# Fewer, wider filler products in the opening, and a new order of stores, loads and conversions in block 1

## The chip, the cores and the metric

The kernel runs on one core of a Trainium2 chip. A core has five engines that run at the same time: PE (TensorE, matrix products; its weight loads are listed as PEld), DVE (VectorE), ACT (ScalarE), POOL (GpSimd) and SP (SyncE, which here only issues DMAs). Each has its own instruction stream, in order, and they wait for one another by semaphores. Data comes from HBM by DMA. PE works from SBUF and writes to PSUM, which has few banks.

The metric is the device time of one execution in microseconds (us).

## The reference

Two layers, one after the other. The first is a retention recurrence over 4 batches, 8 heads, 768 steps and a head size of 64:

```python
for t in range(S):
    state = gamma * state + einsum('bhd,bhe->bhde', k[:, :, t], v[:, :, t])
    y[:, :, t] = scale * einsum('bhd,bhde->bhe', q[:, :, t], state)
```

Its output, seen as x with 3072 rows (tokens) and 512 columns, goes through a dense layer of width 2048 with the Mish activation and back to 512:

```python
h = x @ w_in
g = h * tanh(softplus(h))
out = g @ w_out
```

q, k, v, both weights and the output are 32-bit floats; the kernel computes in 16 bits with 32-bit sums.

## The kernel before

The 3072 rows are cut into 24 chunks of 128 steps. Block 0 has four chunks, each of the ten later blocks two (`BLOCKS`, `first`): block 1 has chunks 4 and 5, block 2 has 6 and 7, block 3 has 8 and 9, block 4 has 10 and 11. For a block, PE computes the products of the recurrence (scores L431 and outer products L438, later L519), then the first dense layer (`g1`, L608, eight steps u = 0 to 7 for a block of two), then the second (`seven`, L811: seven products of half matrices in place of eight, from sums of the operands that DVE makes in `sums_a`, `sums_b` and `sums_c`). The recurrence of the next blocks is woven in between: `get_ready(blk + 1)` is called behind step u = 5 of `g1` in blocks 1 to 3 and gives PE the outer products and scores of the next block (for chunks 8 and 9 that is in block 2).

What a chunk needs before PE can take it:

- `load`: three DMAs of 256 KB on SP's queue (q, k, v, L143). `load_to(g)` loads all chunks below g that are not yet loaded.
- `casts_qk` and `casts_v`: three scaled conversions to 16 bits on POOL (L376, L379, L384). `cast_to(g)` does them for all chunks below g not yet converted; `ncast` counts.
- `turn_by_dma`: a transposing DMA of the converted q and k (L389), issued by SP, which waits for POOL. It writes `qkt`, which scores read. `turn_next(g)` is `cast_to(g + 1)` and then `turn_by_dma(g)`; `turn_load(g)` is `turn_next(g)`, `turn_next(g + 1)` and `load_to(g + 4)`; `turn_both(g)` does both chunks of a block and ends with `load_to`.

The order is written by hand. Every engine gets its instructions in the order in which the program calls them, and SP is a single queue: what stands behind a DMA that waits, waits too. Outputs are collected in `stores` with a due step, and `store_due(u)` at the head of step u issues those that are due (L198). Output tiles `osb` have five buffers; block 0 makes four (`g2_out`), each later block two (`seven`), and a buffer is free again when its store has landed.

In block 1, `plan_of(1)` hangs `turn_next(8)` behind step u = 0 and `load_to(11)` behind u = 1. In `seven`, `cast_behind(1, 2)` follows `sums_b`: POOL first copies one element of the third sum (`summed`, L1119), so that it waits for DVE, and then converts chunks. Hooks in `seven` then issue the transposes.

The opening (`first_block`) starts with DMAs for the first q, k and v. Until those land and are converted PE has nothing of its own, and `spin(n, per)` gives it products of an identity matrix with itself (L402) into a PSUM tile that is overwritten later: n times 128 columns, `per` times 128 columns in one product, and `per` is 4 if it isn't given. The opening's own work is: turns by PE (`turn_first_q`, `turn_pair`, L219) which DVE or ACT copy to SBUF (L223, L225), scores (L294) that DVE masks (L299), outer products (L312), and the sums of both (L339, L348).

Of the kernel before, what the change touches and what calls it, by code (L numbers as in the profile page):

```python
# [16 lines left out]
def kernel(  # L17
# [20 lines left out]
    first = [sum(BLOCKS[:i]) for i in range(len(BLOCKS))]  # L38
# [82 lines left out]
    ONE, MIX = 3, 6  # L121
    nload, ncast = [0], [0]
# [22 lines left out]
    def load(g):  # L145
        room(g)
        for n in range(3):
            load_one(g, n, nc.sync)

    def load_to(g):  # L150
        while nload[0] < min(g, NCK):
            load(nload[0])
            nload[0] += 1
# [73 lines left out]
    def turn_first_q(qf, a, on_act):  # L227
        n = H // 2
        q16 = castp.tile([P, CPB, n, D], FP16, name="qk16", bufs=4)
        nc.vector.tensor_tensor(  # L230
            q16.rearrange("p r h d -> p h r d"), qf[:, a * n:(a + 1) * n],
            qs_four[:, a * n:(a + 1) * n].unsqueeze(3).broadcast_to((P, n, CPB, D)),
            op=ALU.mult)
        qt = qktp.tile([P, HP // 2, CPB, P], FP16, name="qkt", bufs=6)
        turn_parts(lambda i, r: q16[:, r, 2 * i:2 * i + 2], qt, on_act)
        first_q.append(qt)
# [29 lines left out]
    def turn_pair(n, nm, a, on_act):  # L266
        if a == 0:
            pairs[n, nm + "t"] = qktp.tile([P, HP, 2, C], FP16, name="qkt", bufs=6)
        t = pairs[n, nm, a]
        turn_parts(lambda i, r: t[:, r, 2 * i:2 * i + 2],  # L270
                   pairs[n, nm + "t"][:, a * (HP // 2):(a + 1) * (HP // 2)], on_act)
# [98 lines left out]
    def casts_qk(g):  # L370
        qf, kf, _ = loaded[g]
        qk16 = castp.tile([P, 2, H, D], FP16, name="qk16", bufs=4)
        q16, k16 = qk16[:, 0], qk16[:, 1]
        v16 = castp.tile([P, H, D], FP16, name="v16", bufs=7)
        heads = slice(g % 2 * (H // 2), (g % 2 + 1) * (H // 2))
        nc.gpsimd.tensor_tensor(  # L376
            q16.rearrange("p (r h) d -> p h r d", r=2), qf,
            qs_two[:, heads].unsqueeze(3).broadcast_to((P, H // 2, 2, D)), op=ALU.mult)
        nc.gpsimd.tensor_tensor(  # L379
            k16, kf, boosts.unsqueeze(2).broadcast_to((P, H, D)), op=ALU.mult)  # L380
        cast[g] = (q16, k16, v16, qk16)

    def casts_v(g):
        nc.gpsimd.tensor_tensor(  # L384
            cast[g][2], loaded.pop(g)[2], vs[g % 2].unsqueeze(2).broadcast_to((P, H, D)), op=ALU.mult)
# [11 lines left out]
    def spin(n, per=HP):  # L397
        at = pairs[min(x for x in pairs if type(x) is tuple and x[1] == "at")]
        to = at.rearrange("p h i r c -> p h (i r) c")
        for i in range(0, n, per):  # L400
            m = min(per, n - i)
            nc.tensor.matmul(  # L402
                to[:, 0, :m], ident, ident.unsqueeze(1).broadcast_to((P, m, P)),
                start=True, stop=True)
# [215 lines left out]
    def g2_mm(o_ps, blk, t, fb, cols=slice(None)):  # L620
        s, f = divmod(fb, FPS)
        nc.tensor.matmul(  # L622
            o_ps, gts[blk, fb][:, t * P:(t + 1) * P], wouts[s][:, f, cols],
            start=(fb == 0), stop=(fb == NFB - 1))

    def out_rows(blk, t):
        if blk == 0:
            return out[:TB].rearrange("(p r) c -> r p c", r=CPB)[t]
        row0 = (first[blk] + t) * P
        return out[row0:row0 + P]  # L630

    def g2_out(o_ps, t, due):
        osb = op.tile(list(o_ps.shape), FP32, name="osb", tag="osb")
        if t == 0:
            nc.scalar.copy(osb, o_ps)
        else:
            nc.vector.tensor_copy(osb, o_ps)
        stores.append((due, out_rows(0, t), osb))
# [265 lines left out]
    def first_block():  # L904
# [9 lines left out]
        pair_at(0, 0)  # L914
        spin(46, 1)
        turn_first_q(qf, 0, True)
        spin(14, 1)
        turn_first_q(qf, 1, False)
        for n in range(2):
            for a in range(2):  # L920
# [5 lines left out]
                base=0, pattern=[[-1, 2], [-2, D // 2]], channel_multiplier=1)  # L926
        keep_from(keep_two, 2, [[1, 2], [-1, 2], [-2, D]])
        turn_pair(0, "k", 0, True)
        spin(8, 1)
        pair_scores(0, 0)  # L930
        pair_at(0, 1)
        turn_pair(0, "k", 1, True)
        spin(8, 1)
        pair_scores(0, 1)
        turn_pair(1, "k", 0, True)
        cast_pair(0, "v", 0)
# [60 lines left out]
        def sum_weights(half, n):  # L997
# [5 lines left out]
        plan = {  # L1003
            9: [(cast_wout, 0)],
            12: [(cast_wout, 1)],
            16: [(cast_wout, 2), (load_more,), (cast_qk,)],
            17: [(sum_weights, 0, 3)],
            23: [(cast_wout, 3, True)],
            25: [(turn_two,)],
            26: [(pair_scores, 2, 0)],  # L1010
            27: [(pair_scores, 2, 1)],
# [5 lines left out]
        o_tiles = [None] * CPB  # L1017
        for u in range(2 * NFB):
            if u < 2:
                if u == 0:  # L1020
                    open_in(2)
            elif u < NFB:
                g1(0, u)
            elif u < 2 * NFB - 2:
                w = u - NFB
                if w == 0:
                    for t in range(CPB):
                        pool, tag = (pxps, "px") if t == 0 else (mmps, "mm")
                        o_tiles[t] = pool.tile([P, d_model], FP32, name="o_ps", tag=tag)
                for t in range(CPB):  # L1030
                    if t == CPB - 1 and w == 1:
                        g2_mm(o_tiles[t], 0, t, 0)
                    if t < CPB - 1 or w > 0:
                        g2_mm(o_tiles[t], 0, t, w)
            else:
                for t in range(CPB // 2) if u % 2 == 0 else range(CPB // 2, CPB):
                    for w in range(NFB - 2, NFB):
                        g2_mm(o_tiles[t], 0, t, w)
                    g2_out(o_tiles[t], t, 1)
            for fn, *args in plan.get(u + 1, ()):  # L1040
                fn(*args)

# [30 lines left out]
    def turn_both(g):  # L1073
        for n in range(2):
            casts_qk(g + n)
            turn_by_dma(g + n)
        for n in range(2):
            casts_v(g + n)
        ncast[0] = g + 2
        load_to(g + 4)  # L1080

    def next_chunk(g):
        turn_next(g)
# [32 lines left out]
    def cast_behind(blk, i):  # L1116
        g = first[blk] + (6 if blk == 1 else 8)
        if ncast[0] < min(g, NCK):
            nc.gpsimd.tensor_copy(summed, gsums[blk % 2][:, i, NFB // 2 - 1, P - 1:])  # L1119
            if blk + 1 >= MIX:  # L1120
                cast_to(g - 2)
                casts_qk(g - 2)
                ncast[0] = g
            else:
                cast_to(g)
# [5 lines left out]
    def plan_of(blk):  # L1131
        a = first[blk] + 4
        plan = {u: [] for u in (0, 1, 4, 5, 7)}
        if tight(blk):
            plan[5] = [(get_ready, blk + 1)]
        elif blk < MIX:
            plan[0] = [(settle, blk + 1), (mask_two, blk + 1), (leave, blk + 1)]
        if blk == 1:
            plan[0] += [(turn_next, a)]
            plan[1] += [(load_to, a + 3)]  # L1140
        elif blk < ONE:
            plan[1] += [(next_chunk, a)]
            plan[4] += [(load_to, a + 4)]
        return plan

    first_block()
    for blk in range(1, len(BLOCKS)):
        last = blk + 1 == len(BLOCKS)
        plan = plan_of(blk)
        if blk >= MIX:  # L1150
            second_of(blk - 1)
            mixed_in(blk, last)
        elif blk > ONE:
            weight_left.extend(in_sums(blk - ONE - 1))
        for u in range(NFB // 2 if blk < MIX else 0):
            store_due(u)
            g1(blk, u)
            if u in ((6, 7) if tight(blk) else (5, 7)):
                sums_a(blk, u // 7)
            for fn, *args in plan.get(u, ()):  # L1160
                fn(*args)
            if weight_left:
                weight_left.pop(0)()
        hooks = [[], [], []]
        if not last:
            later = blk + 2 if ONE <= blk < len(BLOCKS) - 2 else None
            hooks = [[(retain, blk + 1, later, True)],
                     [(next_one, first[blk] + 6)] if blk + 1 >= MIX else
                     [(next_two, first[blk] + 6, tight(blk))] if blk >= ONE else
                     [(turn_next, first[blk] + 5), (load_to, first[blk] + 8)] if blk == 1 else  # L1170
                     [(next_chunk, first[blk] + 5), (turn_load, first[blk] + 6)],
                     [(finish, blk + 1)] if later is None else []]
        if tight(blk):
            hooks[2].append((leave, blk + 1))
        seven(blk, [(mask_two, blk + 1)] if tight(blk) else [], hooks, last)
# [31 lines left out]
```

## Time and profile before

| what | us |
|---|---|
| median of 3 runs | 199.38 |
| all three | 199.31, 199.38, 200.82 |
| the profiled execution's own time | 200.37 |
| its span, first to last instruction | 198.6 |

| engine | busy us | share of the span | instructions |
|---|---|---|---|
| PE | 190.2 | 96% | 2999 |
| PEld | 154.8 | 78% | 2999 |
| DVE | 129.8 | 65% | 246 |
| ACT | 99.1 | 50% | 182 |
| POOL | 73.7 | 37% | 97 |

The profile is of one execution. Times in it count from the span's start. A row of a timeline gives start, length, engine, line and operation, output and inputs, shape and the number of merged instructions; in brackets stands how long the engine was idle before it, and what released it. "issue" there means that the engine waited for nothing that the profile shows. In the chain of waits each row is a start, a length and what the time went to. PE's products are pipelined and their ends are modelled, so distances from start to start are the surer measure.

The DMA engines are busy for 90% or more of nearly all slices up to 145 us.

### The profile page before, as it was taken

Reading aid. Unit: us, or ns where it says so; the run is one execution under the profiler, and the core shown is the slowest. Engines: PE = TensorE matmul, PEld = TensorE weight load, DVE = VectorE, ACT = ScalarE, POOL = GpSimd, SP = SyncE. Lnnn points to the kernel's source line nnn. Section 1 sums busy time; section 2 is a strip of 40 time slices with the busy share of each in tenths; the row PEclk is TensorE's granted clock in tenths of the full one; section 3 lists DMA queues with packets and bytes.
Section 4 is the critical chain, followed back from the end, with each engine's and each line's share of the span. In section 5 each row is a group of like instructions: output and inputs, shape, how many; then the busy total and the mean of one; then the engine's idle time right before and its main releaser. Section 6 shows DMA issues by size and latency. Waiting matters only on the chain.

```text
span 198.6 us, 6893 instructions
## 1 busy us (share of the span) xinstructions
PE 190.2 (96%) x2999; PEld 154.8 (78%) x2999; DVE 129.8 (65%) x246; ACT 99.1 (50%) x182; POOL 73.7 (37%) x97
## 2 busy tenths in 40 slices
PE   7799999999999999999799999999999999999993
PEld 7566444545887888888688888998998998988982
DVE  0688433988597269266946766866885884867462
ACT  2377673243642542554364464484484664763750
POOL 6562000659267603953905704434525710000000
PEclk9999999999999999999999999999999999999999
DMA  6999999999799999999999999879994250300202
GB/s 179 302 315 349 371 384 353 312 293 176 171 229 290 240 223 274 140 117 256 275 160 299 169 178 270 80 187 254 95 236 89 54 156 5 109 3 3 106 26 79
DMA packets 84141, 38.75 MB, mean 195 GB/s; under 512 B 57744, under 2 KB 78736, under 8 KB 84112
## 3 DMA queue, kind: packets, MB, share of 16 engines
q1 hardware_dynamic: 83968, 38.28, 82.2%
q8 instruction: 23, 0.38, 0.9%
q10 hardware_dynamic: 144, 0.05, 0.2%
q14 instruction: 6, 0.05, 0.1%
HBM read 27.31 MB, written 6.29 MB: 169 GB/s over the span
## 4 chain that ended last, share of the span: by engine, by line
PE 87%; DMA 5%; POOL 2%; DVE 2%; issue 2%; SPq 1%; ACT 1%; DVEq 0%; POOLq 0%
PE o_ps L811 29%; PE h_ps L608 23%; PE h_ps L738 9%; PE h_ps L718 8%; PE o_ps L622 7%; PE y_ps L519 3%; DMA kf<-in_k_dram 3%; DMA out_dram<-osb 2%; PE u_ps L438 1%; PE at L431 1%; PE t_ps L219 1%; PE at L294 1%; PE h_ps L593 1%; DVE am L299 1%; POOL v L384 1%
## 5 line engine op out<-in xcount | busy, mean ns | idle before, releaser
L608 PE MATMUL h_ps<-xt,win 128*128 128x256 f16 (+1 forms) x376 | 48.9, 289 | 1.3 <-issue 1.3
L616 ACT ACTIVATE g<-h_ps 128x512 f16<-128x512 f32 x54 | 32.3, 597 | 27.4 <-PE h_ps L608 27.4
L608 PEld LDWEIGHTS <-win 128*128 128x128 f16 x376 | 36.4, 98 | 12.1 <-issue 1.7
L811 PEld LDWEIGHTS <-gsum 128*128 128x128 f16 x320 | 30.1, 98 | 4.5 <-DVE gsum L681 0.7
L811 PE MATMUL o_ps<-tmat,gsum 128*128 128x256 f16 x240 | 29.4, 273 | 0.0
L811 PEld LDWEIGHTS <-g 128*128 128x128 f16 x240 | 23.2, 98 | 3.0 <-issue 0.4
L376 POOL TENSOR_TENSOR qk<-qf,qvs 128x512 f16<-128x512 f32 x18 | 19.5, 1083 | 8.7 <-DMA qf<-in_q_dram 4.7
L817 ACT COPY snap<-o_ps 128x256 f32<-128x256 f32 x30 | 11.2, 372 | 20.1 <-PE o_ps L811 20.1
L738 PE MATMUL h_ps<-xt,win 128*128 128x256 f16 x160 | 20.7, 273 | 0.0
L379 POOL TENSOR_TENSOR qk<-kf,qvs 128x512 f16<-128x512 f32 x18 | 19.7, 1093 | 0.0
L384 POOL TENSOR_TENSOR v<-vf,qvs 128x512 f16<-128x512 f32 x18 | 19.4, 1088 | 0.0
L811 PE MATMUL o_ps<-wout,g 128*128 128x256 f16 x160 | 19.1, 273 | 0.0
L825 DVE TENSOR_TENSOR osb<-o_ps,snap 128x256 f32<-128x256 f32 x30 | 12.7, 423 | 9.7 <-ACT xt L573 3.3
L1119 POOL COPY summed<-gsum 128x1 f16<-128x1 f16 x7 | 1.7, 245 | 40.6 <-DVE gsum L677 26.5
L738 PEld LDWEIGHTS <-win 128*128 128x128 f16 x160 | 14.8, 98 | 1.4
L573 ACT CAST xt<-y_ps 128x512 f16<-128x512 f32 x15 | 10.1, 731 | 10.9 <-PE y_ps L519 10.9
L729 ACT ACTIVATE g<-h_ps 128x512 f16<-128x512 f32 x25 | 14.2, 588 | 2.4 <-PE h_ps L738 2.4
L622 PE MATMUL o_ps<-wout,g 128*128 128x512 f16 x64 | 15.0, 380 | 0.0
L753 DVE TENSOR_TENSOR hsum<-h_ps,hsum 128x512 f32<-128x512 f32 x15 | 10.4, 692 | 6.1 <-PE h_ps L718 4.4
L748 ACT COPY hsum<-h_ps 128x512 f32<-128x512 f32 x15 | 8.8, 586 | 10.8 <-PE h_ps L718 10.8
L672 DVE TENSOR_TENSOR gsum<-g 128x512 f16<-128x512 f16 x20 | 9.1, 457 | 7.4 <-ACT g L616 5.3
L475 DVE TENSOR_TENSOR mid<-u_ps,sth 128x256 f16<-128x256 f32 x15 | 6.3, 422 | 9.8 <-PE u_ps L438 9.5
(97 smaller groups left out, 290.0 us busy)
## 6 DMA issues: line engine op xcount, KB each, us to landing
kf<-in_k_dram SPq DMA_DIRECT2D x24, 256.0 KB, 5.3
vf<-in_v_dram SPq DMA_DIRECT2D x24, 256.0 KB, 5.5
out_dram<-osb SPq DMA_DIRECT2D x22, 256.0 KB, 3.7
qf<-in_q_dram SPq DMA_DIRECT2D x20, 256.0 KB, 5.0
wi<-in_moe_w_in_dram SPq DMA_DIRECT2D x6, 512.0 KB, 8.5
wt<-in_moe_w_out_dram SPq DMA_DIRECT2D x3, 1024.0 KB, 10.4
qfirst<-in_q_dram SPq DMA_DIRECT2D x2, 512.0 KB, 4.5
wi<-in_moe_w_in_dram SPq DMA_DIRECT2D x1, 1024.0 KB, 10.0
```

The lines of the kernel that those rows point to most:

```text
L376: nc.gpsimd.tensor_tensor(q16.rearrange("p (r h) d -> p h r d", r=2), qf, qs_two[:, heads].unsqueeze(3).broadcast_to((P, H // 2, 2, D)), o ...
L379: nc.gpsimd.tensor_tensor(k16, kf, boosts.unsqueeze(2).broadcast_to((P, H, D)), op=ALU.mult)
L384: nc.gpsimd.tensor_tensor(cast[g][2], loaded.pop(g)[2], vs[g % 2].unsqueeze(2).broadcast_to((P, H, D)), op=ALU.mult)
L608: nc.tensor.matmul(h_ps[:, j], wins[s][f // 2][:, bp, f % 2 * P:(f % 2 + 1) * P], xts[blk][:, bp, :nt], start=(bp == 0), stop=(bp == NBP - 1))
L616: nc.scalar.activation(gt, h_ps, AF.Mish, scale=inv_boost3)
L622: nc.tensor.matmul(o_ps, gts[blk, fb][:, t * P:(t + 1) * P], wouts[s][:, f, cols], start=(fb == 0), stop=(fb == NFB - 1))
L718: nc.tensor.matmul(o_ps[:, f], w(f // 2, k)[:, f % 2 * P:(f % 2 + 1) * P], x[:, k], start=begin and f == 0 and k == 0, stop=k == 1, skip_g ...
L729: nc.scalar.activation(to, src, AF.Mish, scale=inv_boost3)
L738: nc.tensor.matmul(h_ps[:, f], wins[w][h // 2][:, k, h % 2 * P:(h % 2 + 1) * P], xts[blk][:, k, :2 * C], start=k == 0, stop=k == NBP - 1)
L811: nc.tensor.matmul(o_ps, x(f), w(f), start=first and z == 0, stop=z == n - 1, skip_group_check=True)
L817: nc.scalar.copy(x, o_ps)
L825: nc.vector.tensor_tensor(dst, o_ps, plus, op=ALU.add)
```

## The change

In the opening, three calls of `spin` take wider products: 14 products of 128 columns become 7 of 256, and twice 8 products of 128 become 2 of 512. The columns are the same, and there are 19 products, each with its weight load, fewer.

In block 1: block 0's four stores are due at step 0, not 1. `turn_both(6)` loads up to chunk 8 and not up to 9, and chunk 9 is loaded behind the stores, at step 0, in place of `turn_next(8)`. So chunk 8 is neither converted nor transposed there. `cast_behind(1, 2)` converts q and k of chunks 8 and 9 and then v of both, all behind the third sum; before, it converted chunk 9 alone. The hook that transposed chunk 9 now transposes 8 and 9. Nothing that is computed changes.

```diff
         turn_first_q(qf, 0, True)
-        spin(14, 1)
+        spin(14, 2)
         turn_first_q(qf, 1, False)
...
         turn_pair(0, "k", 0, True)
-        spin(8, 1)
+        spin(8)
         pair_scores(0, 0)
         pair_at(0, 1)
         turn_pair(0, "k", 1, True)
-        spin(8, 1)
+        spin(8)
         pair_scores(0, 1)
...
-                    g2_out(o_tiles[t], t, 1)
+                    g2_out(o_tiles[t], t, 0)
...
     def turn_both(g):
...
         ncast[0] = g + 2
-        load_to(g + 4)
+        load_to(g + 3)
...
     def cast_behind(blk, i):
...
             nc.gpsimd.tensor_copy(summed, gsums[blk % 2][:, i, NFB // 2 - 1, P - 1:])
-            if blk + 1 >= MIX:
+            if blk == 1:
+                for n in range(g - 2, g):
+                    casts_qk(n)
+                for n in range(g - 2, g):
+                    casts_v(n)
+                ncast[0] = g
+            elif blk + 1 >= MIX:
...
     def plan_of(blk):
...
         if blk == 1:
-            plan[0] += [(turn_next, a)]
+            plan[0] += [(load_to, a + 2)]
             plan[1] += [(load_to, a + 3)]
...
-                     [(turn_next, first[blk] + 5), (load_to, first[blk] + 8)] if blk == 1 else
+                     [(turn_load, first[blk] + 4)] if blk == 1 else
```

## The prediction

> **What bounds the kernel now.** The page first: PE is busy for nearly the whole span at full granted clock, so only time in which PE issues nothing can be won.
>
> ```profile
> PE 190.2 (96%) x2999; PEld 154.8 (78%) x2999; DVE 129.8 (65%) x246; ACT 99.1 (50%) x182; POOL 73.7 (37%) x97
> ...
> q8 instruction: 23, 0.38, 0.9%
> ```
>
> The second line is a DMA queue that carries the program itself: 23 packets, 0.38 MB, so 16 KB each. PE has 2999 products and 2999 weight loads; 5998/23 is 261 instructions a packet, so a packet is one block of 256 (64 bytes each).
>
> Next I went through PE's timeline for places where one product starts late after another. After 17 us only three exceed 0.2 us. Two are idle on "issue", on nothing that the profile shows:
>
> ```profile
> 21.11 3.18 PE L608 MATMUL h_ps<-xt,win 128*128 128x512 f16 x14 [0.20 <-issue]
> ...
> 97.02 1.25 PE L608 MATMUL h_ps<-xt,win 128*128 128x256 f16 x10 [1.08 <-issue]
> ```
>
> Counting by stretches tells what they are. The columns to read are PE's and PEld's (x), instructions since the start:
>
> ```profile
> 0.00:20.95 20.95, 17.26 (x351) 13.45 (x352) 12.14 (x17) 10.77 (x22) 10.05 (x29) 1.00 1.00 289
> 0.00:96.50 96.50, 91.81 (x1375) 66.92 (x1376) 60.24 (x97) 44.52 (x80) 45.00 (x64) 1.00 1.06 263
> ```
>
> Between the stops lie 1375-351 = 1024 products and 1024 loads, exactly 8 blocks. Queue 8's packets lie at 18.50 to 19.62 and 94.29 to 95.57 us; PE goes on 1.49 and 1.45 us after their ends. I read this as PE at the end of a block whose successor is late. Block ends thus lie at 704 and 2752 instructions and every 256 between. A block is fetched once its predecessor's start is crossed: instruction 448 is crossed at 14.28, its packet comes at 18.50; 2496 is crossed at 91.14, packet 94.29. The DMA engines are full there (share 1.00 and 1.06), and the packet waits 3 to 4 us.
>
> The third stop is in block 1. The chain of waits:
>
> ```profile
> 56.87 1.23 POOL v L384
> 58.10 0.41 SPq L389
> ...
> 58.59 4.43 DMA out_dram<-osb
> ...
> 63.15 0.43 DVE osb L825
> 63.59 0.04 issue
> 63.63 1.03 PE o_ps L811 x8
> ```
>
> osb has five buffers; block 0 fills four. DVE's second osb of block 1 needs the first store landed (63.03), PE's next product needs the PSUM bank that DVE reads, and SP issued the store at 58.59 only because chunk 8's transpose stood ahead of it, waiting for POOL.
>
> By start-to-start distance (a 128x256 product normally follows after 0.109 us, a 128x512 after 0.216) the stops cost 0.580-0.216 = 0.36, 0.526-0.109 = 0.42 and 1.352-0.109 = 1.24 us: 2.02 together. The idle times in brackets (0.20, 0.26, 1.08: 1.54) are the lower account, since they begin at modelled ends.
>
> **The opening.** 14 products of 128 columns become 7 of 256, twice 8 become 2 of 512: the same columns, 19 products and 19 loads fewer. They fill waits: the 14 take 0.94 us from 6.61 and the next work waits for DVE until 7.52; each 8 take 0.61 us, over 0.2 us before ACT's qkt. Seven products of 256 take 7 x 0.109 = 0.76, and the trace's pair of 128x512 takes 0.59 (11.80). Directly this is 0.
>
> Indirectly everything behind them moves 38 instructions against the block ends. At the 97 us stop the end now falls 19 products later, 19 x 0.109 = 2.07 us, while the block is asked for 0.15 us later (instruction 2534 of before, 91.29). The missing 1.24 us becomes a reserve of 2.07-0.15-1.24 = 0.68. At 21 us the end falls 19 x 0.216 = 4.1 us later and the request 0.84 (15.12 against 14.28): reserve 2.9. The same sum for every later block, with before's own packet delays, leaves 1.2 us or more at all others. The tight one is the first: end 448 is reached at about 15.1, asked for when end 192 is crossed, in the spin at 9.7 to 10.2. With that packet's delay in before (9.65 to 11.81, 2.2), its length 1.19 and the 1.45 behind it, code is there at 14.5 to 15.1. Just in time, and PE's work there has 0.3 us of cover (idle before 16.66 for DVE's mid). I take 0; the bounds are 0 and the rival below.
>
> The Trainium skill (Runtime: NRT & Kernel Launch, Instruction fetch mechanics) gives the 16 KB blocks of 256 instructions, which agrees with the rows, and calls the crossing of a boundary mostly hidden, which the 1.08 us idle contradicts. By that rule the shift would be worth nothing and the sum 0.42.
>
> **Block 1: stores ahead.** SP's order becomes load 8, four stores, load 9, load 10, transposes 8 and 9. Block 0's osb are written by 50.1, so the stores go at about 53.4, behind load 8, and land about 4.4 us later, 58 to 60. The 0.42 goes (bounds 0.26 by idle, 0.42 by starts; I take 0.42, the issue distance). What is late next there: PE's 61.95 row waits for DVE's mask at 61.91, 0.09 us over the usual step. Load 9 is moved past four stores (2.19 us of SP) and lands at 60 to 62 instead of 57.67 to 59.94; POOL needs its q at 62.7, k at 63.7. Load 10 no longer waits behind transpose 8: 57.5 instead of 60.84.
>
> **Chunk 8 behind the third sum.** POOL no longer converts at 54.85 to 58.09. DVE's f16 sums beside that took 1.04 and 1.15 us where the same lines took 0.41 and 0.42 next; up to 1.3 us of DVE time comes free. PE waited little on DVE there: 0 to 0.1, I take 0. POOL then does q8, k8, q9, k9, v8, v9, six of about 1.05 from 60.7 to 66.8, or 0.8 earlier with the rest. Consumers: block 3's products for chunks 8 and 9 (L438 69.83, L431 70.11), now about 0.8 earlier. v9 has 2 us of reserve. Transpose 9 can issue when k9 is done, about 64.1, behind transpose 8; with before's 3.1 to 5.2 us from issue to landing it lands at 67.2 to 69.3, chunk 9's scores need it at about 69.5. Hidden; without cover up to 2 us. Chunk 10's conversion starts 0.8 us later than at 65.99, but its transpose waits on SP until 69.71 anyway, and its user comes at 85.
>
> **Sum.** 0.36+0.42+1.24 = 2.02 off the profiled execution's 200.37 (span 198.6, 1.77 around it) if the late block's reserve holds: 198.35. The runs without a profile are 199.31, 199.38 and 200.82: two are 1 us below the profiled one, a spread as large as the fetch stop itself. If their stop at 97 us is the shorter by that 1 us, they win only 0.36+0.42+0.24 = 1.0. So the gain lies between 1.0 and 2.0; I take 1.6 and go from the median, 199.38, to 197.8.
>
> **Rivals.** *The stops are not fetches, or reappear elsewhere*: then only the store's part is won, 199.0. The 1024 = 4 x 256 products between them speak against it; that only two of 22 block ends stall speaks for chance.
> The Trainium skill's rule above leads here too.
>
> *The first fetch comes late*: with the second packet's delay (4.2 instead of 2.2 us), because weight loads of larger packets are ahead of it, code comes at 16.9 instead of 15.1. The opening then ends about 1.5 us later: 197.8+1.5 = 199.3.
> *Slower: transpose 9.* Both transposes are issued back to back behind load 10. Elsewhere, behind full queues, the issue alone took 3 to 4.2 us and landing 6.2 (114.17 to 120.37). Then transpose 8 holds SP to about 66.3, transpose 9 lands at 72.5, and PE waits 3.0 us in block 2 for chunk 9: 197.8+3.0 = 200.8. It decides from a landing later than 69.5, and it turns the result above before from 71.1. Against it: load 10 now lands by about 65, so the queue is shorter than at 114 us.
> Measurement tells about 1% (2 us) from no change, so my forecast is near that line: faster than 197.39 needs nearly the full 2.0.
>
> **Chances.** Forecast 0.60, no fetch gain 0.15, late first fetch 0.10, transpose 9 0.15. Of the forecast half lies below 197.39 (0.30); of transpose 9 a third is over 201.37, and 0.03 is for a program or DMA effect that I don't see: slower 0.08, same 0.62. The forecast's own range is 197.2 to 198.6. To leave out 0.2 I go down to 197.0 and up to 199.7, which takes in no fetch gain and the late first fetch, not the full transpose wait.
>
> **What would show it.** Right: no "issue" idle at PE near 21 and 97 us; stores issued near 53.4 us, no DVE wait for out_dram in block 1; block 4's first product about 2 us earlier than 97.02. Wrong: an "issue" idle at another block end, above all near 15 us; PE idle at L431 near 69.5 with DMA qkt as its releaser; later blocks that give the time back at L431 near 120, where the qkt transpose issued at 114.17 landed (120.37) only 1.4 us ahead of its first reader (121.77).

## The result, and the profile after

The changed kernel takes 0.9943 of the time of the kernel before, with a 95% interval of 0.9926 to 0.9960 (20 runs of each): medians 199.09 us against 200.12, a gain of 0.57% or 1.14 us. One run of the 20 took 246.0 us, at a granted clock of 0.759, and is left out of the ratio, as are a few runs of this kind in the ratios below. The forecast was 197.8 us, a gain of 1.6 us from 199.38. The sign is right. The gain is 0.7 of what was forecast, and it stands clear of no change, which the forecast had called hardly measurable.

The profiled execution took 198.83 us, its span 197.1 (before 200.37 and 198.6). The first lines are from the page's busy times, queues and groups (busy us, mean ns of one, idle time before them); the last is the same group in the page of before:

```profile
PE 190.6 (97%) x2980; PEld 154.7 (78%) x2980; DVE 128.6 (65%) x246; ACT 99.1 (50%) x182; POOL 74.2 (38%) x97
...
q8 instruction: 23, 0.38, 0.8%
...
L608 PE MATMUL h_ps<-xt,win 128*128 128x256 f16 (+1 forms) x376 | 48.5, 289 | 0.0
...
L608 PE MATMUL h_ps<-xt,win 128*128 128x256 f16 (+1 forms) x376 | 48.9, 289 | 1.3 <-issue 1.3
```

19 products and 19 weight loads are gone, and PE's busy time has not changed by more than 0.4 us: nothing was won by doing less. What has gone is idle time. The group of L608 waited 1.3 us on "issue" before, and now 0.0.

PE's timeline (start, length, line, shape, number of merged instructions, idle time before and its releaser) answers the rows at 21, 63.6 and 97 us:

```profile
19.17 3.19 PE L608 MATMUL h_ps<-xt,win 128*128 128x512 f16 x14
...
62.91 1.04 PE L811 MATMUL o_ps<-tmat,g 128*128 128x256 f16 x8
...
94.65 5.51 PE L608 MATMUL h_ps<-xt,win 128*128 128x256 f16 x49
```

None has a bracket: the two stops on "issue" and the one behind the store are gone. The same timeline shows where two shorter ones came:

```profile
15.03 0.62 PE L348 MATMUL y_ps<-qkt,mid 64*64 64x128 f16 x5 [0.28 <-ACT seen L954]
15.42 0.22 PE L312 MATMUL u_ps<-v,qk 64*64 64x64 f16 x2
...
84.98 0.38 PE L431 MATMUL at<-qkt 64*64 64x64 f16 x24 [0.27 <-DMA qkt<-qk]
```

Between 15.10 and 15.40 us no product starts, 0.26 us beyond the usual step of 0.06; the gap lies within the first row's merged five, and so it has no bracket. The table by stretches says which instruction is late (PE and PEld with their counts, in the stretch from 0):

```profile
0.00:15.20 15.20, 12.54 (x223) 9.59 (x224) 7.94 (x9) 6.96 (x13) 8.83 (x27) 1.00 0.96 266
```

223 + 224 = 447, so the late one is instruction 448, the first block end that the prediction called tight. Queue 8's packet lay at 12.87 to 14.06 us; PE went on 1.34 us after its end. The other new wait, at 84.98, is for the transpose of chunk 11: 0.43 us from start to start. Its cause stands on SP's queue and in the chain of waits:

```profile
77.58 2.36 SPq L143 DMA_DIRECT2D vf<-in_v_dram  x1
80.04 2.85 SPq L389 DMA_TRANSPOSE qkt<-qk  x1
```

```profile
78.96 1.09 POOL v L384
80.04 4.89 DMA qkt<-qk
84.94 0.04 issue
84.98 0.38 PE at L431 x24
```

The chain names POOL's conversion of v as what came before the transpose, but the transpose needs only k, which POOL had done at 78.96. SP's row is the truer reading: it issued the load of v of chunk 13 until 79.94, and the transpose stood behind it.

**Accounts.** Every profile can be cut at layer one's first product (the first `h_ps`). A stop is counted here where a product starts over 0.12 us later behind the one before it than it does at the same place in most profiles. The rest of the span behind the first product, less these stops, is nearly the same in all kernels of this study:

| kernel | first product at | rest | stops in the rest | difference |
|---|---|---|---|---|
| before | 17.23 | 181.34 | 0.37 + 0.42 + 1.24 = 2.03 | 179.31 |
| before, second profile | 17.60 | 180.19 | 0.26 + 0.38 + 0.30 = 0.94 | 179.25 |
| before, third profile | 17.63 | 180.10 | 0.23 + 0.61 = 0.84 | 179.26 |
| changed | 17.30 | 179.76 | 0.43 | 179.33 |
| changed, second profile | 18.07 | 178.99 | none | 178.99 |

So the time goes where these stops are, and nowhere else to within 0.3 us; half of that is a wait of 0.17 us at L811 near 108 us, which the changed kernel's second profile lacks and the other four have. The mean of the stops is 1.27 us before and 0.22 after, 1.05 less. The first product comes 0.2 us later, and the spans are 0.97 us shorter on the mean. The runs give 1.14 us, with 0.80 to 1.48 as the interval: the accounts agree, as closely as three and two profiles can.

### The profile page after: what moved, and what is told of

The parts are those of the page before. It is cut to its first block, busy times and chain, and to the rows that moved or that the text cites. A ratio compares the mean times of both kernels' runs of the same rounds, so it can differ in the third digit from the quotient of the medians.

```text
span 197.1 us, 6854 instructions
## 1 busy us (share of the span) xinstructions
PE 190.6 (97%) x2980; PEld 154.7 (78%) x2980; DVE 128.6 (65%) x246; ACT 99.1 (50%) x182; POOL 74.2 (38%) x97
## 4 chain that ended last, share of the span: by engine, by line
PE 88%; DMA 5%; POOL 2%; ACT 1%; issue 1%; SPq 0%; DVE 0%; POOLq 0%
PE o_ps L811 31%; PE h_ps L608 21%; PE h_ps L738 9%; PE h_ps L718 8%; PE o_ps L622 7%; PE y_ps L519 4%; DMA kf<-in_k_dram 3%; DMA qkt<-qk 2%; PE at L431 2%; PE u_ps L438 1%; PE t_ps L219 1%; PE h_ps L593 1%; PE at L294 1%; ACT qkt L223 1%; PE y_ps L348 1%
## 5 line engine op out<-in xcount | busy, mean ns | idle before, releaser
L608 PE MATMUL h_ps<-xt,win 128*128 128x256 f16 (+1 forms) x376 | 48.5, 289 | 0.0
L608 PEld LDWEIGHTS <-win 128*128 128x128 f16 x376 | 36.4, 98 | 10.5 <-DVE xt L364 0.4
L811 PEld LDWEIGHTS <-gsum 128*128 128x128 f16 x320 | 30.1, 98 | 4.5 <-DVE gsum L681 0.7
L811 PE MATMUL o_ps<-tmat,gsum 128*128 128x256 f16 x240 | 29.4, 273 | 0.0
L811 PEld LDWEIGHTS <-g 128*128 128x128 f16 x240 | 23.3, 98 | 2.6
L811 PE MATMUL o_ps<-wout,g 128*128 128x256 f16 x160 | 19.1, 273 | 0.0
L672 DVE TENSOR_TENSOR gsum<-g 128x512 f16<-128x512 f16 x20 | 8.5, 426 | 7.2 <-ACT g L616 5.1
```

The costliest lines, as they stand in the source:

```text
L608: nc.tensor.matmul(h_ps[:, j], wins[s][f // 2][:, bp, f % 2 * P:(f % 2 + 1) * P], xts[blk][:, bp, :nt], start=(bp == 0), stop=(bp == NBP - 1))
L811: nc.tensor.matmul(o_ps, x(f), w(f), start=first and z == 0, stop=z == n - 1, skip_group_check=True)
```

## The experiments

**The two parts alone.** Both start from the kernel before.

```diff
 e1_opening: the opening alone
-        spin(14, 1)
+        spin(14, 2)
...
-        spin(8, 1)
+        spin(8)
...
-        spin(8, 1)
+        spin(8)
 e2_block1: all of the change but these three lines
```

> The kernel before with the three wider spins alone, block 1 as before. Theory A (the idle times on issue near 21 and 97 us are PE at the end of a 256-instruction block whose successor is late, and the spins move all later work by 38 instructions): both are gone, a short stop of 0.1 to 0.4 us appears near 15 us where instruction 448 now lies, the wait for out_dram near 63 us stays (0.3 to 0.45), chunk 11's transpose lands over 0.8 us ahead of its first reader near 84.8. Span 197.0 to 197.4 against 198.6; time 0.5 to 0.8% below the kernel before. Theory B (the stops are not program blocks, the gain of the change is block 1's): both stops stay, time within 0.15% of before.

> The changed kernel with the three spins put back to narrow products: block 1's new order alone. Theory A: the stops on issue near 21 us (0.2) and 96 us (about 1) stay, the wait for out_dram in block 1 is gone (0.4 won from start to start), and PE waits 0.1 to 0.5 us for chunk 11's qkt in L431 near 85 us, because SP is about a microsecond later behind two transposes back to back. Time within 0.25% of before. Theory B: 0.4 to 0.6% below before, like the whole change.

The opening alone gave 0.9992 (0.9959 to 1.0025), block 1 alone 1.0018 (0.9992 to 1.0043). Neither part is worth anything that these runs show; together they are worth 0.57%.

In block 1 alone the instruction counts are those of before, and the stops at 21 and 97.6 us stayed, 0.20 and 0.69 us. The wait for the store went, as it should. But the wait for chunk 11's transpose is there, longer than in the changed kernel:

```profile
86.35 0.38 PE L431 MATMUL at<-qkt 64*64 64x64 f16 x24 [1.19 <-DMA qkt<-qk]
```

From start to start 1.35 us: more than the store's part had won.

In the opening alone the stops at 21 and 97 went, so the shift by 38 instructions does what was said. DVE still waited for the store in block 1 (1.1 us in the table of waits), yet PE didn't stop there. Instead two transposes were late. PE's timeline and the chain in block 2:

```profile
121.22 0.22 PE L431 MATMUL at<-qkt 64*64 64x64 f16 x2 [0.50 <-DMA qkt<-qk]
```

```profile
63.23 1.45 SPq L143
64.68 0.05 issue
64.73 0.03 SPq L389
64.76 0.03 issue
64.79 5.37 DMA qkt<-qk
70.15 0.04 issue
70.19 0.38 PE at L431 x24
```

Chunk 9's transpose stands behind loads of chunk 10 that SP needed until 64.68 to issue; it landed at 70.15 and cost PE 0.27 us. The one at 121.22 (chunk 17) cost 0.66. PE came to both earlier than before, because stops ahead of them were gone, but the transposes also landed later. Counted from layer one's first product, PE came to chunk 9's at 52.1 us (52.4 to 52.9 in three profiles of the kernel before) and it landed at 52.4 (51.1 to 51.5); for chunk 17 the times are 102.7 (103.3 to 104.5) and 103.4 (102.2 to 103.1).

**Moving the block ends the other way.** If the stops at 21 and 97 us are ends of program blocks, they must fall on the same instruction number whatever the work is. This kernel is the one before with 19 products of 64 columns more behind `spin(46, 1)`:

```diff
         spin(46, 1)
+        spin_small(19)    # 19 products of 64 x 64 x 64 of the identity matrix
```

> The kernel before with 19 products of 64x64 (and their 19 weight loads) added behind the 46 of the opening, where PE idles 0.76 us: they take 19 x 27 ns = 0.5 us of it. All later work moves by 38 instructions the other way. Theory A: block end 704 now lies in the first products of layer one (L593, near 18 us), 19 products earlier, and its code comes at 20 to 21 us as before: a stop of 1.5 to 2.7 us there; the stop of 97 us moves to the last products of block 3 (L811, near 94 us) and lasts 0.4 to 1.5 us; ends with little reserve (near 109 and 138 us) may stop for up to 0.6. Time 0.7 to 1.5% above before. Theory B: the stops stay at the same products and the time within 0.2% of before.

The time was 1.0221 (1.0175 to 1.0268): 204.92 us against 200.09, for 19 of the smallest products in a place where PE waits anyway. PE's timeline (the lines quoted here are 7 higher than in the kernel before):

```profile
20.88 1.36 PE L600 MATMUL h_ps<-xt,win 128*128 128x256 f16 x11 [2.65 <-issue]
...
96.78 0.49 PE L818 MATMUL o_ps<-wout,gsum 128*128 128x256 f16 x3 [0.72 <-issue]
...
142.90 0.33 PE L725 MATMUL h_ps<-xt,win 128*128 128x128 f16 x3 [0.53 <-issue]
```

The table by stretches, up to just ahead of each:

```profile
0.00:20.80 20.80, 15.40 (x351) 12.99 (x352) 11.93 (x16) 9.12 (x18) 10.01 (x29) 1.00 0.99 286
0.00:96.50 96.50, 90.58 (x1375) 66.39 (x1376) 58.48 (x92) 44.02 (x79) 43.07 (x62) 1.00 1.02 256
0.00:142.60 142.60, 136.16 (x2143) 106.44 (x2144) 90.73 (x161) 66.96 (x121) 62.81 (x84) 1.00 1.02 240
```

351 and 1375 are the counts of the kernel before, to the product, though each now falls 19 products earlier in the program: at 20.88 us on L600 (L593 before) where it was L608, and at 96.78 on layer two's L818 (L811) where it was layer one. The third, 2143, is 768 = 6 x 128 products on, again whole blocks. A fourth stop, of 0.13 us at 113.36, has 1631 products ahead of it, 256 more than the second. Ahead of the three shown, queue 8's packets ended at 19.41, 95.28 and 141.35 us, each 1.47 to 1.55 us before PE went on, as in the kernel before (1.49 and 1.45). That the stops are block ends is thereby shown. Their lengths are 2.82, 0.88, 0.13 and 0.70 us from start to start, 4.53 together; the rest less these is 179.17, as in the table above. That profile is the fastest of six runs; the others paid more, for a reason told at the end.

**Chunk 11's transpose ahead of the load.** The changed kernel, with q and k of chunk 13 loaded first, then the transpose of chunk 11, then v:

```diff
+            elif blk == 2:
+                cast_to(g - 2)
+                turn_by_dma(g - 3)
+                load_one(g - 1, 2, nc.sync)
+                nload[0] = g
+                cast_to(g)
...
-            plan[4] += [(load_to, a + 4)]
+            plan[4] += [(load_qk, a + 3)]
...
-                     [(next_chunk, first[blk] + 5), (turn_load, first[blk] + 6)],
+                     [(turn_load, first[blk] + 6)],
```

> The changed kernel with one swap on SP: chunk 11's transpose goes ahead of the load of chunk 13's v, which held SP in the changed kernel from 77.58 to 79.93 us while POOL was done with chunk 11's k at 78.96. If the wait of PE at 84.98 us for qkt (0.43 from start to start) is owed to that queue, the transpose is issued at 79.0 and lands at 82.0 to 83.8, the wait is gone, and the time is 0.15 to 0.25% below the changed kernel (0.7 to 0.85% below before). If the transpose is slow by the DMA engines alone, it lands after 84.4 all the same and nothing is won. Against it: v of chunk 13 lands about 1 us later (85), and POOL needs it at 85.1.

> The changed kernel with chunk 11's transpose ahead of the load of chunk 13's v, once more, beside the changed kernel on one chip: no wait for qkt near 85 us, and 0.1 to 0.3% below the changed kernel. If the two agree within 0.1%, the wait of 0.43 us in the changed kernel's profile is not what its runs pay on average.

> The changed kernel once more, beside the other three on one chip: 0.4 to 0.7% below before, PE's wait for chunk 11's qkt near 85 us between 0 and 1.3 us by execution.

The ratio was 0.9928 (0.9901 to 0.9955), and in a second set of runs 0.9919 (0.9892 to 0.9945), with the changed kernel beside it at 0.9914 (0.9882 to 0.9946). The wait is gone in both profiles. Counted from layer one's first product, SP issued the transpose at 61.57 us in both, instead of 62.74 in the changed kernel's first profile, and PE passed L431 without an idle time. But the changed kernel's second profile doesn't have the wait either: its transpose was issued at 61.57 too, when POOL had done k, since the load ahead of it held SP for 1.19 us there and not for 2.36. The medians of the second set are 198.83 and 198.72. So the order removes a wait that the changed kernel pays only in some runs, and no gain over the changed kernel is shown.

**Half of block 1.** The opening with the stores ahead of load 9 but chunk 8 handled as before, and the opening with chunk 8 behind the third sum but the stores where they were:

```diff
 e5_stores: e1_opening, and
-                    g2_out(o_tiles[t], t, 1)
+                    g2_out(o_tiles[t], t, 0)
...
-        load_to(g + 4)
+        load_to(g + 3)
...
-            plan[0] += [(turn_next, a)]
+            plan[0] += [(load_to, a + 2), (turn_next, a)]
 e6_defer: e1_opening, and
-            plan[0] += [(turn_next, a)]
...
+            if blk == 1:        # q, k of 8 and 9, then v of both, as in the change
...
-                     [(turn_next, first[blk] + 5), (load_to, first[blk] + 8)] if blk == 1 else
+                     [(turn_load, first[blk] + 4)] if blk == 1 else
```

> The wider spins and block 0's stores ahead of load 9, but chunk 8 converted and transposed at step 0 as before and chunk 9 alone behind the third sum. If the stores' place is what block 1 is worth: no wait for out_dram, like the changed kernel, 0.4 to 0.7% below the kernel before. If the place of the transposes on SP is what counts: DVE's f16 sums beside POOL at 56 us stay at 1.0 us, chunk 9's transpose stands behind load 10 and lands at 68.8 to 70.2, and PE waits up to 0.5 us for it in L431 near 69.5; 0.1 to 0.4% below before.

> The wider spins and chunk 8 converted with chunk 9 behind the third sum, but load 9 ahead of block 0's stores and the stores due at step 1, as before. No transpose stands before the stores any more, so they go at about 56.0 us and land at 60 to 61, ahead of DVE's second osb at 61.8: no wait for out_dram in this kernel either. If so, the stores' own new place is worth nothing beside the deferral: time within 0.15% of the changed kernel (0.4 to 0.75% below before). If landing comes after 62 the wait stays in part and the time is 0.1 to 0.2% worse than the changed kernel.

The ratios were 0.9940 (0.9918 to 0.9963) and 0.9948 (0.9921 to 0.9975). With the opening, neither half can be told from the whole (0.9943, and 0.9914 with 0.9882 to 0.9946 beside these runs). Neither profile has a stop of PE behind the opening (rest 179.20 and 179.21). Either takes the transpose of chunk 8 away from ahead of the stores: in the second SP issued them at 57.31 though they still stand behind load 9, against 59.29 in the opening alone. What differs is DVE. With the stores alone POOL still converts beside its sum of halves, and its timeline has one long one:

```profile
56.44 0.96 DVE L672 TENSOR_TENSOR gsum<-g 128x512 f16<-128x512 f16 x1
57.43 0.42 DVE L673 TENSOR_TENSOR gsum<-gsum,g 128x512 f16<-128x512 f16 x1
```

In the changed kernel all four sums of this kind take 0.41 to 0.43. PE didn't wait for it in either.

**Repeats.** Since single profiles differed by a microsecond in the same program, the opening alone and the kernel before were profiled again.

> The kernel before with the wider spins alone, once more. If what block 1 takes back in this kernel (PE's waits for qkt of chunks 9 and 17 in L431, 0.27 and 0.66 us in its first profile) is usual, its time is again within 0.3% of before, and its profile has a wait for qkt in L431 near 70 us. If the first result was chance: 0.4 to 0.8% below before, like the changed kernel.

> The kernel before, one more profile. The stops on issue lie at the same products as in the first (the 352nd and the 1376th), since the program decides where a block ends; their length is the DMA queues', and I expect 0 to 0.4 us at the first and 0.2 to 1.3 us at the second. From layer one's first product to the end: 180.2 to 181.4 us (first profile 181.34, changed kernel 178.99 to 179.76).

> The kernel before, a third profile, for how much the two stops and the wait for out_dram vary: stops at the same products, wait for out_dram 0.2 to 0.5 us from start to start, rest of the program behind layer one's first product 180.2 to 181.4 us.

The opening alone gave 0.9958 (0.9941 to 0.9976) this time; the two intervals overlap only between 0.9959 and 0.9976, so it may be worth a little. That it is worth less than the whole change is what the first set says; the second set's interval includes the whole's 0.9943. Its second profile has waits of 0.21 us at 70.21 (chunk 9) and 0.23 at 85.50 (chunk 11).

The kernel before took 199.58 and 199.50 us in these two profiled executions. At 97 us the third profile shows

```profile
96.20 2.02 PE L608 MATMUL h_ps<-xt,win 128*128 128x256 f16 x17 [0.45 <-issue]
```

which is 0.61 us from start to start, and the second 0.30. With 0.69 from block 1 alone, whose program lies on the same instruction numbers, the stop priced at 1.24 has four sizes: 1.24, 0.69, 0.61 and 0.30, mean 0.71. The one at 21 us has 0.37, 0.26, 0.23 and 0.20, mean 0.27. The one behind the store has 0.42, 0.38 and, in the third, none (DVE waited 0.9 us there, PE didn't).

**More of the same.** If fewer and wider products are good, and the blocks' first fetch has cover, 23 fewer again should do no harm. The changed kernel with

```diff
-        spin(46, 1)
+        spin(46, 2)
```

> The changed kernel with the opening's first 46 products of 128 columns as 23 of 256 too: the same columns at the half clock of the first microseconds, 46 more instructions fewer. By the block ends the first one (instruction 448) moves on by 0.8 us of PE's work, and its request, when instruction 192 is crossed, by 1.2 us or more, into the turns at 11.4 to 12.1: the code then comes at 17.0 to 18.6 and PE stops for 1.0 to 2.5 us near 16 us. All later ends keep over 1 us of reserve. From the first conversion of k to layer one's first product 10.8 to 12.2 us against 9.95 to 10.33 in the other kernels, and the time 0.2 to 0.8% above the changed kernel (0.1% above to 0.5% below before). If fewer, wider products were good by themselves, it would be at or below the changed kernel.

The ratio was 1.0099 (1.0065 to 1.0133), 202.33 us against 200.12: the change's gain of 1.1 us is lost and 2.2 us more. PE's timeline:

```profile
18.28 0.27 PE L312 MATMUL u_ps<-v,qk 64*64 64x64 f16 x4 [2.09 <-issue]
```

That is again instruction 448. By the prediction's reading the block that it begins is asked for when 192 is crossed, which the 23 products fewer put from about 10.2 us to about 12.1; the packet came at 15.79 to 16.93 instead of 12.87 to 14.06, and PE went on 1.35 us after it. The stop of 2.28 us then had a second price, told at the end.

## Why the prediction was right and wrong

**What bounds the kernel** held for the change: PE stayed at 97%, and only its stops changed the time. In the two kernels that moved the block ends further PE's clock changed it too, as told at the end.

**The block ends** held. The reserves that the shift was to give were 2.9 and 0.68 us; with 1.45 us behind the packets' ends (20.68 and 95.17 us) and instructions 704 and 2752 at 25.00 and 97.60, they are 2.9 and 1.0 in the changed kernel. What did not hold is "A block is fetched once its predecessor's start is crossed": in the same trace of before a packet began at 51.44 us, and instruction 1216, whose crossing should have asked for it, started on PE at 52.51. The request can go out ahead of that start, and what it hangs on isn't shown. By the Trainium skill (Runtime: NRT & Kernel Launch, Instruction fetch mechanics) crossing a block's end is mostly hidden. Here it cost 4.53 us in one profile with 19 products more, 2.28 in one with 23 fewer, and about 1 us on the mean in the kernel before. The block of 256 instructions that the same section names agrees with all counts. The rival that the stops aren't fetches is refuted by the same two kernels.

**The sum failed**, in this step: "So the gain lies between 1.0 and 2.0; I take 1.6". The term that was mis-sized is the 97 us stop, "1.352-0.109 = 1.24". It was read off one profile, and it was the largest of four: the mean is 0.71. With means the three terms are 0.71 + 0.27 + 0.27 = 1.25 (the store's over its three profiles), where 2.02 stood. The working held the warning, since two runs were 1 us below the profiled one and the lower end, 1.0, came from that; the middle was taken between the longest stop of four and the usual ones. Two costs that the sum put at nothing, the first fetch and chunk 11, came to 0.2 us each on the mean.

**The chances failed** in "Measurement tells about 1% (2 us) from no change". With 20 runs of each the interval is 0.17% to either side, so 0.57% is a clear gain. That the time would most likely stay within 1% was right as a size; that such a change can't be told from none was wrong. The start also counted: 199.38, the median of three runs, became 200.12 with twenty. Of the 1.29 us between 197.8 and 199.09, 0.74 is that, and 0.55 the gain.

**The first fetch** was to be "Just in time", at a cost of 0. It came 0.26 us late in the first profile and 0.50 in the second (with the split order 0.18 and 0.24). From the first conversion of k on POOL to layer one's first product it took 10.05 and 10.33 us, against 10.03, 9.96 and 9.96 before: on the mean 0.2 us. Of the eight profiles with this opening, two had no such wait at all (the opening alone in its second profile, and the one with the stores alone), so this cost too varies from run to run. The rival of 1.5 us was right in the place and too large here; with 23 products fewer it came in full.

**Stores ahead.** Forecast: issued at about 53.4, landing 58 to 60, and 0.42 won. The first was issued at 52.10, they landed at 57.89 to 59.82, and no DVE wait for `out_dram` stands in block 1. The step that the store had to move ahead of load 9 isn't borne out: taking chunk 8's transpose from ahead of it was enough. The prediction's chain names POOL's v ahead of that transpose, but it needs only q and k: SP began to issue it at 56.93, when k was done, and took until 58.50.

**Chunk 8 behind the third sum.** DVE's sums fell from 1.04 and 1.15 to 0.41 and 0.43 us, and PE won nothing by it, as said. Chunk 9's transpose was issued at 66.10 and landed at 69.27, the top of the forecast 67.2 to 69.3; its first reader came at 69.46. The slower rival (72.5, 3.0 us) was 0.2 us of reserve away from beginning, and in the opening alone, where the transpose isn't moved, it did begin: 0.27 and 0.21 us.

**Chunk 11** is the step whose cover was wrong: "its transpose waits on SP until 69.71 anyway, and its user comes at 85". Behind chunk 10 stands chunk 11, with its transpose behind load 13 on SP, and the user at 85 is its own. In the trace of before it had landed at 83.67, 0.8 us ahead of 84.5, where PE now reaches that place; in the changed kernel it landed at 84.94. The give-back was forecast near 120 us, and it was at 85: 0.43 us in one profile, none in the other, 1.35 in block 1 alone. At 120 nothing came in the changed kernel, but 0.66 did in the opening alone.

**Block 4's first stretch** was to start about 2 us earlier than 97.02. The product that stands there in the program (the 1376th before, the 1357th now) starts at 95.5: 1.5 us earlier, which is the 2.03 of stops less the new 0.43 and 0.07 of a later first product.

**Why the parts don't add up.** Each part takes stops away ahead of a transpose that has little reserve. The opening alone brings PE earlier to the transposes of chunks 9, 11 and 17, which still stand behind loads and land later than before; block 1 alone keeps the fetch stops and delays chunk 11. Together, chunk 9 lands in time and the fetch stops are gone. These waits are seen in the profiles; that they make up the difference between the opening (0.9992 and 0.9958) and the whole (0.9943 and 0.9914) in the runs isn't shown, because stops vary from run to run by as much and only one or two profiles of each kernel exist.

**What stays open** is why two delays vary so from run to run. One is how long a load or a transpose holds SP and takes to land: in the changed kernel chunk 11's transpose landed 4.90 us after its issue in one profile and 4.10 in the other. The other is the delay of a block's packet, which sets the length of the stop: in the four profiles whose stops at 97 us were 1.24, 0.69, 0.61 and 0.30 us, the packet ended 4.43, 3.89, 3.72 and 3.50 us after PE had started instruction 2496. The DMA engines are full near these places (shares of 1.00 to 1.06), and no run here took that load away.

## What to carry to other kernels

Where a kernel's busiest engine stops on nothing that the profile shows, count its instructions up to the stop: if two such counts lie a whole number of program blocks apart, the work isn't the cause, and a few instructions more or fewer far ahead of it move the stop or remove it, in either direction (19 small products more cost 2.2%, part of it by the clock, 19 fewer helped to win 0.6%, 42 fewer cost 1.0%). Price a stop of this kind by several profiles of the same program and not by the one at hand. When a stop goes, list the transfers behind it that have less reserve than the stop was long, and do so for each one on the same queue, not only for those that the change moves.

## What the runs showed of the hardware

A late block can cost more than its own wait. During the 2.09 us of idle time with `spin(46, 2)` the granted clock fell to half. The table by stretches (the column behind POOL's is the granted clock):

```profile
17.60:24.20 6.60, 5.66 (x78) 4.31 (x78) 4.03 (x8) 1.50 (x4) 0.00 (x0) 0.50 1.08 361
24.40:31.00 6.60, 6.60 (x32) 3.01 (x31) 3.18 (x5) 4.70 (x8) 0.00 (x0) 1.00 1.05 388
```

It was low from about 17.4 to 24.2 us, 6.8 us, and products of 256 columns followed each other after 0.213 us where 0.109 is usual. From layer one's first product to block 1's, block 0 took 33.05 us in that kernel and 31.39 in the changed one's second profile, 1.66 more, and the rest of 180.84 less that is 179.18, as everywhere. Behind the stop of 2.82 us in the profile with 19 more, between 18 and 20.9 us, the same products followed after 0.109 us, at full speed.

Whether a stop has this second price differs from run to run of one program. With `spin(46, 2)` one run of six, at a mean granted clock of 0.998, took 200.85 us; four at 0.989 to 0.991 took 202.13 to 202.51, and the profiled one, at 0.983, took 203.43. With 19 products more two runs at 1.00 took 202.97 and 203.16, and four at 0.983 to 0.991 took 204.84 to 205.59. So about 2 us of that kernel's 2.2% are the clock. Without it the stops explain the time: 200.09, less the 1.27 us of stops in the kernel before, plus 4.53, is 203.3, and the two runs at 1.00 took 0.2 to 0.4 us less.

The Trainium skill (TensorE: Matmul & The Clock Gate, Part 1) gives a window of about 3.4 us that runs freely, after one of which without activity the clock is halved. The half and the length, twice 3.4, agree with the trace, and a free-running window would fit one stop being hit and the other not; but PE had been idle for only some 1.2 us when the clock fell, which is less than a window.

A transposing DMA holds SP for very different times: 1.29 us for chunk 10's in the opening alone, 3.32 for chunk 9's in the same profile. What stands behind it on SP inherits that.
